# Attention, a dense layer and an expert layer in one planned kernel: V read in place, masks by sequence rows, early loads on two queues, and a searched table of due dates

## The chip, the cores and the metric

The kernel runs on one core of one Trainium2 chip. The metric is the device time of one launch in microseconds; the kernel before was run three times, and the median counts. Beside these runs stands one profiled execution, whose trace is read below. TensorE is called PE here, VectorE DVE, ScalarE ACT, GpSimd POOL and SyncE SP, as the profile calls them.

## The reference

Three layers follow each other. `_attn_ref` is a linear attention with a decaying state: batch 4, 8 heads, 768 positions, head size 48.

```python
for t in range(S):
    cur = einsum(u * k[t], v[t]);  y[t] = r[t] @ (state + cur)
    state = w[..., None] * state + outer(k[t], v[t])
```

`_moe_ref` is a dense layer on the 3072 tokens of 384 features: `softplus(x @ w_in) @ w_out` with 2048 hidden features. `_moe2_ref` gives every token to one of 8 experts: the scores `x @ w_gate` are taken in falling order and each expert holds 384 tokens; each expert computes `relu(x @ w1) @ w2` with 1024 hidden features.

## The kernel before

**The tiling.** Attention goes in 24 steps, each of 64 positions of two batches at once (128 partitions, 8 heads). A step loads K, R and V (`load_step`, L366, six DMAs into `KN`, `RN`, `VN`, each with two buffers), multiplies K and R by tables of the decay's powers (`PWN`), transposes both on PE (`tk` L497, `tq` L501), forms the 64x64 products of queries and keys (`prods`, L524), masks them (`masked`, L532 and L537), adds to the state (`fresh`, L558), and multiplies by V and by the state (`outs`, L607). For `outs` the masked products and the queries lie one above the other in a buffer `AR`, and V and the state lie one above the other in a buffer `X`, so that one matmul of 128 rows does both. V comes into `X` by copies from `VN` in the first six steps (`COPIED`), and by two more DMAs from memory later. The term with u is made by `sums` on PE (L591, with `rkT` from DVE, L586) in the first six steps (`TURNED`), and by four DVE operations (`bonus`) later. The result of the step (`xf`, L612) is transposed on PE (`tx`, L620) in the first six steps, and by a DMA transpose (`turn`, L623) later.

Three steps make a block of 384 tokens; there are eight. `ffn1` (L730) multiplies a block by w_in in 16 pieces (block 0 in float32, L743; the others in three float16 products, L748), and softplus runs on ACT and DVE. `ffn2` (L855 in float32 for block 0, L858 to L860 later) multiplies by w_out, which carries the gate's columns too. `late_logits` (L785, L786) makes the scores of the last tokens by small matmuls. Then the selection of the experts' tokens runs on DVE with small matmuls, and for each expert POOL gathers its rows, DMA transposes turn them (L1334), SP loads its weights in pieces (`mraw`, L1294), ACT and DVE split them, PE multiplies (L1346, then L1364 to L1366), and POOL scatters the result (L1374).

**The planner.** Nothing runs in the order in which it is written. Each piece of work is an `Item` with an engine (or a choice between ACT and DVE), an expected duration, its dependences and a due date. `lay_out` (L148) plays the program through with these durations before it is built: on each engine it takes, among the items that could start within `SLACK` of the earliest, the one that is due first, and the engines' instruction lists come out in that order. A transfer is an item of SP with a size in ns: its data are taken to land 1000 ns after a single serial DMA resource has worked off that size. Where the plan leaves PE idle, `keep_warm` (L135) writes matmuls on a tile of zeros, `still`, into PE's list (L143). They are instructions like all others: their number is fixed when the kernel is built.

```python
k = int((it.start - last - 100.0) / step)   # step: 107 ns before the first piece of work, 56 ns after
```

## Time and profile before

| what | value |
|---|---|
| three runs | 746.02, 747.25, 748.87 us; median 747.25 us |
| the profiled execution | 747.23 us, span of the trace 745.5 us |
| PE, DVE, ACT, POOL busy | 730.9, 610.0, 399.1, 61.2 us |
| granted TensorE clock, mean | 0.995 of 2.4 GHz |
| DMA | 79.06 MB, mean 106 GB/s |

The span runs from the first instruction's start to the last one's end; the profiled execution's own time is 1.7 us longer. A busy PE is one with a matmul in it; the matmuls on `still` count as busy, and overlap of neighbouring matmuls makes the busy time of one line longer than the time by which it moves the next one. That second time is read from the starts of two rows of a timeline.

### The profile page before, as it was taken

What the parts mean: (1) busy time and instruction counts of PE and PEld (TensorE: products, weight loads), DVE (VectorE), ACT (ScalarE), POOL (GpSimd) and SP (SyncE); (2) the same over time, 40 slices, a digit from 0 to 9 for tenths busy, and PEclk for the clock granted to TensorE, in tenths of its full rate; (3) what the DMA queues carried; (4) which work ended last, traced back from release to release, by engine and by line L of the source; (5) the groups of instructions that cost most, each with busy time, mean ns of one, the idle gap of its engine ahead of it and who ended that gap; (6) DMA issues with size and microseconds to landing.
All of it is one profiled execution on the core that took longest, in us unless ns stands there. A gap on an engine that the chain in (4) does not pass through costs nothing.

```text
span 745.5 us, 18249 instructions
## 1 busy us (share of the span) xinstructions
PE 730.9 (98%) x7196; PEld 475.0 (64%) x7196; DVE 610.0 (82%) x1663; ACT 399.1 (54%) x803; POOL 61.2 (8%) x100
## 2 busy tenths in 40 slices
PE   8899999999999999999999999999999999999996
PEld 7766666666666666667766665655655565656663
DVE  6899999999888788789998967887799799987530
ACT  4586776776565565667989901211235435433531
POOL 2000000000000000000001000000213312323211
PEclk9999999999999999999999999999999999999998
DMA  5796776135333233233110003342347647766910
GB/s 106 182 205 170 172 178 149 24 65 111 73 67 71 53 67 66 54 66 64 34 23 11 2 12 107 107 121 61 96 117 223 175 129 213 209 159 189 220 56 32
DMA packets 165013, 79.06 MB, mean 106 GB/s; under 512 B 130496, under 2 KB 160576, under 8 KB 164928
## 3 DMA queue, kind: packets, MB, share of 16 engines
q1 hardware_dynamic: 161856, 68.46, 39.6%
q0 software_dynamic: 3072, 9.44, 3.8%
q8 instruction: 56, 0.92, 0.5%
q14 instruction: 29, 0.24, 0.1%
HBM read 60.37 MB, written 9.83 MB: 94 GB/s over the span
## 4 chain that ended last, share of the span: by engine, by line
PE 68%; DVE 13%; issue 9%; ACT 3%; DMA 3%; POOL 2%; SPq 1%; POOLq 0%; DVEq 0%
PE bank L748 18%; PE bank L1346 8%; PE bank L858 7%; PE bank L860 7%; PE bank L859 7%; PE bank L855 3%; PE bank L607 2%; PE bank L1364 2%; PE bank L1365 2%; PE bank L1366 2%; PE bank L743 1%; DMA mraw<-moe_w 1%; DVE gf L761 1%; PE bank L524 1%; PE bank L558 1%
## 5 line engine op out<-in xcount | busy, mean ns | idle before, releaser
L748 PEld LDWEIGHTS <-wi 128*128 128x128 f16 x1008 | 97.8, 98 | 65.4 <-issue 2.0
L748 PE MATMUL bank<-xt,wi 128*128 128x384 f16 x672 | 127.6, 326 | 0.0
L754 ACT ACTIVATE ta<-bank 128x384 f32<-128x384 f32 x128 | 62.0, 484 | 65.4 <-PE bank L748 52.9
L858 PE MATMUL bank<-wo,g 128*128 128x384 f16 (+1 forms) x240 | 79.2, 330 | 0.0
L761 DVE SCALAR_TENSOR_TENSOR gf<-bank,ta 128x384 f32<-128x384 f32 x112 | 61.5, 550 | 21.6 <-ACT ta L756 20.8
L860 PE MATMUL bank<-wo,g 128*128 128x384 f16 (+1 forms) x240 | 79.1, 330 | 0.0
L859 PE MATMUL bank<-wo,g 128*128 128x384 f16 (+1 forms) x240 | 79.1, 329 | 0.0
L748 PE MATMUL bank<-xs,wi 128*128 128x384 f16 x336 | 72.9, 326 | 0.0
L1346 PE MATMUL bank<-g,w1h 128*128 128x384 f16 x384 | 72.9, 326 | 0.0
L755 ACT ACTIVATE ta<-ta 128x384 f32<-128x384 f32 x128 | 66.7, 521 | 2.8
L756 ACT ACTIVATE ta<-ta 128x384 f32<-128x384 f32 x128 | 66.7, 521 | 2.6
L1366 PE MATMUL bank<-w2h,g 128*128 128x384 f16 x192 | 62.6, 326 | 0.0
L1364 PE MATMUL bank<-w2h,g 128*128 128x384 f16 x192 | 62.6, 326 | 0.0
L1365 PE MATMUL bank<-w2l,g 128*128 128x384 f16 x192 | 62.6, 326 | 0.0
L1350 ACT ACTIVATE g<-bank 128x384 f16<-128x384 f32 x64 | 31.3, 489 | 44.9 <-PE bank L1346 30.9
L351 ACT ACTIVATE x2o<-bank 128x384 f16<-128x384 f32 x24 | 11.7, 488 | 78.7 <-PE bank L860 62.4
L1346 PEld LDWEIGHTS <-w1h 128*128 128x128 f16 x384 | 35.4, 97 | 23.1 <-issue 1.0
L1353 DVE SCALAR_TENSOR_TENSOR g<-bank,g 128x384 f16<-128x384 f32 x64 | 34.3, 547 | 15.0 <-ACT g L1350 14.9
L768 DVE SCALAR_TENSOR_TENSOR g<-gf,g 128x384 f16<-128x384 f32 x80 | 43.7, 551 | 1.9 <-ACT g L351 1.1
L1346 PE MATMUL bank<-g,w1l 128*128 128x384 f16 x192 | 41.7, 326 | 0.0
L537 DVE TENSOR_TENSOR ar<-bank,mask 64x256 f32<-64x256 f32 x84 | 35.4, 422 | 4.1 <-PE bank L524 2.4
L1269 POOL DMA_INDIRECT third<-x2d,idx x24 | 26.1, 1086 | 146.5 <-DVE si L1186 120.4
(232 smaller groups left out, 1448.8 us busy)
## 6 DMA issues: line engine op xcount, KB each, us to landing
mraw<-moe_w SPq DMA_DIRECT2D x64, 384.0 KB, 4.2
third<-moe_w_in SPq DMA_DIRECT2D x16, 384.0 KB, 4.3
third<-moe_w_out SPq DMA_DIRECT2D x8, 768.0 KB, 4.8
kn<-k SPq DMA_DIRECT2D x48, 96.0 KB, 3.0
rn<-r SPq DMA_DIRECT2D x48, 96.0 KB, 3.4
vn<-v SPq DMA_DIRECT2D x48, 96.0 KB, 3.0
x2d<-x2o SPq DMA_DIRECT2D x48, 96.0 KB, 2.2
X<-v SPq DMA_DIRECT2D x36, 96.0 KB, 3.1
```

Source lines behind the costliest of these rows:

```text
L748: PE.matmul(ph, WF[:, f, a, kk, :], x[:, kk, :], start=(i == 0), stop=(i == 3 * KC - 1))
L754: op("act", 371.0, lambda: ACT.activation(ta, bank.view(BT), AF.Abs), w=[("ta", c)], due=due, bank=bank)
L755: op("act", 413.0, lambda: ACT.activation(ta, ta, AF.Exp, scale=-1.0), w=[("ta", c)], due=due)
L756: op("act", 413.0, lambda: ACT.activation(ta, ta, AF.Ln, bias=1.0), w=[("ta", c)], due=due)
L761: op("dve", 470.0, lambda: DVE.scalar_tensor_tensor(gf, bank.view(BT), 0.0, ta, op0=OP.max, op1=OP.add), r=[("ta", c)], w=[("gf", c)], due ...
L858: PE.matmul(p, gh[:, f, ts], WU[:, f, 0, :no], start=(f == 0), stop=False)
L859: PE.matmul(p, gh[:, f, ts], WU[:, f, 1, :no], start=False, stop=False)
L860: PE.matmul(p, gl[:, f, ts], WU[:, f, 0, :no], start=False, stop=(f == FC - 1))
L1346: PE.matmul(ph, a[:, kk, fs], XH[p][:, x0 + kk, :], start=(i == 0), stop=(i == 3 * KC - 1))
L1364: PE.matmul(po, h1h[:, f, js], w2h[:, fz, :], start=(f == 0), stop=False)
L1365: PE.matmul(po, h1h[:, f, js], w2l[:, fz, :], start=False, stop=False)
L1366: PE.matmul(po, h1l[:, f, js], w2h[:, fz, :], start=False, stop=(f == FB - 1))
```

## The change

Six things are changed together.

1. **Steps 0 to 2** (`DIRECT`) no longer stack V and state. The products of both halves of the heads lie by sequence rows of all 128 partitions, so one mask multiplication of 128x256 per half of the heads takes the place of one of 64x512. `outs` multiplies the masked products by V where the load put it (16 matmuls of 64x48, `VN`), and in steps 1 and 2 adds 8 matmuls of the queries with the state (64x96, `X`, whose unused quarters are zeroed on POOL at the start). The copies of V into `X` fall away in these steps, the transposed queries are copied once instead of twice, and the sum with the u term is two DVE operations instead of one.
2. **Steps 3 to 5** (`TURNED` falls from 6 to 3) make the u term on DVE (`bonus`) and turn their result by a DMA transpose on SP, as the later steps did.
3. **Tables.** The power tables are made in fewer operations, the first products with K and R read them straight from PSUM, and `uw` is made on POOL.
4. **Loads.** Those of steps 0 to 2 (`QUEUES`) may be issued by ACT as well as by SP. R is loaded ahead of K.
5. **Block 0.** Its first eight pieces of `ffn1` (`PARTED`) are cut by step: three times three matmuls of 128 columns instead of three of 384.
6. **The planner.** A transfer now has two numbers by its kind (work of the serial resource, and time to landing after it), and two engines don't read one bank within `LAT` of each other. `SLACK`, `BIAS` and `YIELD0` are new values, and a table `NUDGE` moves the due dates of some 280 of the more than 3000 items of the plan.

The core of the diff (the same exchange of a size for a pair of numbers is left out where it repeats):

```diff
-    SLACK = 115.403
+    SLACK = 92.403
-    BIAS = 1.876
-    YIELD0 = 212.503
+    BIAS = 2.1139999999999994
+    YIELD0 = 118.0
+    ROWS = (610.0, 1850.0)
+    PIECE = (1520.0, 1420.0)
+    EXPERT = (1650.0, 1390.0)
+    GATHER = (620.0, 2400.0)
+    SCATTER = (640.0, 1000.0)
+    TURN = (1370.0, 700.0)
+    TURN2 = (1310.0, 1900.0)
+    NUDGE = {
+        2: 206418, 3: 1000001350, 55: -347751, 60: -114325, 69: 52946, 76: 72329, 90: -194834, 108: -43471, 109: -34113, 115: -1000280590,
...
+            for b in it.banks:
+                for e, t in b.last.items():
+                    if e != eng and eng != "pe":
+                        at = max(at, t + LAT)
...
-                dma = max(start + 1275.0, dma) + it.size
-                it.lat = dma + 1000.0 - it.done
+                dma = max(start + 1275.0, dma) + it.size[0]
+                it.lat = dma + it.size[1] - it.done
...
-    TURNED, TURN = 6, 1700.0
-    WHOLE = 3
+    TURNED = 3
+    DIRECT = 3
+    PARTED = 8
+    QUEUES = 3
...
-        for key, src, store in (("kn", k, KN), ("rn", r, RN), ("vn", v, VN)):
+        for key, src, store in (("rn", r, RN), ("kn", k, KN), ("vn", v, VN)):
             for b in range(2):
-                op("sp", 650.0, lambda b=b, src=src, store=store: SP.dma_start(
-                    store[i][b * 64:(b + 1) * 64], src[b0 + b, :, s0:s0 + C, :].rearrange("h s d -> s h d")),
-                    w=[(key, i, b)], due=due, size=640.0)
+                def load(eng=None, b=b, src=src, store=store):
+                    (ACT if eng == "act" else SP).dma_start(
+                        store[i][b * 64:(b + 1) * 64], src[b0 + b, :, s0:s0 + C, :].rearrange("h s d -> s h d"))
+
+                op({"sp": 650.0, "act": 650.0} if n < QUEUES else "sp", 650.0, load, w=[(key, i, b)], due=due, size=ROWS)
+        if n < DIRECT:
+            return
...
+        if direct:
+            op(FROM_BANK, 0.0, lambda eng: copied(eng, rT, b2.view(HP, 128)), w=[("ar", i, 0), ("ar", i, 1)], due=due + 2, bank=b2)
...
         def masked(q):
+            if direct:
+                DVE.tensor_mul(am[:, q], b3[q].view(HP, 64), mask[:, None, :].to_broadcast([128, HP, 64]))
+                return
...
         def outs():
+            if direct:
+                py = [b.view(H, D) for b in b55]
+                for h in range(H):
+                    for b in range(2):
+                        rows = slice(b * 64, (b + 1) * 64)
+                        PE.matmul(py[b][rows, h, :], am[rows, h % 2, h // 2, :], VN[i][rows, h, :], start=h == 0, stop=h == H - 1 and n % PC == 0)
+                for b in range(2 if n % PC else 0):
+                    for pr in range(HP):
+                        PE.matmul(py[b][b * 64:(b + 1) * 64, 2 * pr:2 * pr + 2, :], rT[:, pr, b * 64:(b + 1) * 64], X[x][:, :, b, pr, :],
+                                  start=False, stop=pr == HP - 1)
+                return
...
+        def part(t, m):
+            ts = slice(t * 128, (t + m) * 128)
+            for kk in range(KC):
+                PE.matmul(bank.view(BT)[:, ts], WF32[f][:, kk, :], X32[:, kk, ts], start=(kk == 0), stop=(kk == KC - 1))
...
-    total = lay_out(items, lambda it: (it.prio, it.n), {"sp": 1000.0, "dve": 900.0}, True)
+    total = lay_out(items, lambda it: (it.prio + NUDGE.get(it.n, 0), it.n), {"sp": 1000.0, "dve": 900.0}, True)
```

What the planner makes of it is seen in the engines' lists. Three places follow; a name's number is its buffer (`kn_93` and `kn_94` are the two buffers of K), and an "x" the count.

**ACT, from the program's start.** Before, its first work after the load of its function table is the copy of a power table out of PSUM:

```order
L241 ACT_TABLE_LOAD
L357 COPY pwn_147<-bank_80 128x512
L357 COPY X_97<-vn_95 64x192
L357 COPY pwn_146<-bank_81 128x512
L357 COPY kT_109<-bank_82 128x512
```

and now:

```order
L287 ACT_TABLE_LOAD
L426 DMA kn_94<-k 64x8x48
L426 DMA rn_91<-r 64x8x48 x2
L426 DMA kn_93<-k 64x8x48
L426 DMA vn_95<-v 64x8x48
L426 DMA rn_92<-r 64x8x48
L426 DMA kn_94<-k 64x8x48
L426 DMA vn_96<-v 64x8x48
L409 COPY kT_110<-ar_112 128x8x32
L409 COPY pwn_146<-bank_80 128x512
```

Eight issues of transfers now stand ahead of the copy of half of a power table, and that copy ahead of the first transposes on PE.

**PE, `outs` of the second step.** Before, in the first step (the later ones are the same), it is one row of 16 matmuls on `X` between `fresh` and the next step's `prods`:

```order
L558 MATMUL bank_84<-vn_96,ks_103 64x48
L558 MATMUL bank_85<-vn_96,ks_103 64x48
L607 MATMUL bank_86<-X_97,ar_111 64x48 x16
L524 MATMUL bank_80<-ar_112,kT_110 64x64
```

and now, in the second step:

```order
L842 MATMUL bank_86<-xt_117,wi 128x128 x3
L184 LDWEIGHTS still
L184 MATMUL bank_87<-still 128x128
L679 MATMUL bank_84<-vn_96,ar_112 64x48
L679 MATMUL bank_85<-vn_96,ar_112 64x48
L682 MATMUL bank_84<-X_98,ar_112 64x96 x4
L682 MATMUL bank_85<-X_98,ar_112 64x96 x4
L661 MATMUL bank_83<-uw,xhl 128x2 x4
```

The first row is a third of a piece of `ffn1` of block 0: it stands ahead of the second step's `outs`, where before no row of `ffn1` stood ahead of the third step's transposes. The matmuls of 64x48 read `vn_96` itself.

**PE, between the last two experts.** Before, the last matmul of one expert and the first of the next have 41 pairs on `still` between them (one is shown):

```order
L1366 LDWEIGHTS g_128
L1366 MATMUL bank_82<-w2h,g_128 128x384
L143 LDWEIGHTS still
L143 MATMUL bank_87<-still 128x128
L1346 LDWEIGHTS w1h
L1346 MATMUL bank_83<-g_129,w1h 128x384
```

and now none:

```order
L1473 LDWEIGHTS g_128
L1473 MATMUL bank_84<-w2l,g_128 128x384
L1474 LDWEIGHTS g_128
L1474 MATMUL bank_84<-w2h,g_128 128x384
L1454 LDWEIGHTS w1h
L1454 MATMUL bank_81<-g_129,w1h 128x384
```

In the whole list of PE, the matmuls on `still` fall from 270 to 183. Up to the first float16 matmul of `ffn1` they were 185 and are 149; from there to the end they were 85 and are 34. Of the other rows, those of `sums` fall from 24 to 12 and those of `tx` from 18 to 9, 24 matmuls of 384 columns become 72 of 128, and 48 of the 384 of `outs` become 48 of 64x48 and 16 of 64x96.

## Rows read from the trace of the kernel before

**Rows 1.** The page: PE's busy time, share and instructions.

```profile
PE 730.9 (98%) x7196; PEld 475.0 (64%) x7196; DVE 610.0 (82%) x1663; ACT 399.1 (54%) x803; POOL 61.2 (8%) x100
```

**Rows 2.** Busy time by stretches, all engines; then clock, DMA share, GB/s.

```profile
0.00:5.00 5.00, 4.00 (x45) 4.00 (x46) 1.53 (x13) 1.28 (x1) 4.16 (x17) 1.00 0.26 39
...
35.00:100.00 65.00, 63.41 (x683) 43.38 (x682) 62.39 (x122) 46.92 (x101) 0.00 (x0) 1.00 0.79 184
```

**Rows 3.** What PE waited for, whole span: us in total, times, longest.

```profile
PE bank L743 <- DVE wi L659: 1.4, 2, 1.0
PE bank L558 <- DVE ks L346: 1.4, 1, 1.4
```

**Rows 4.** Matmuls on `still` (L143) by stretches: length, PE busy (count), PEld busy.

```profile
0.00:6.50 6.50, 4.75 (x55) 4.57 (x55) 1.00 0.39 64
6.50:34.20 27.70, 6.43 (x81) 5.46 (x81) 1.00 0.74 165
34.20:100.00 65.80, 4.70 (x52) 3.43 (x51) 1.00 0.78 182
100.00:400.00 300.00, 4.82 (x22) 2.15 (x22) 1.00 0.34 69
400.00:700.00 300.00, 1.60 (x20) 1.17 (x20) 0.99 0.46 128
700.00:745.50 45.50, 2.45 (x41) 2.37 (x41) 0.96 0.30 72
```

**Rows 5.** Timeline of PE before the last expert: start, length, what.

```profile
712.97 2.45 PE L143 MATMUL bank<-still 128*128 128x128 bf16 x41
...
715.26 1.14 PE L1346 MATMUL bank<-g,w1h 128*128 128x384 f16 x6
```

**Rows 6.** Timeline of SP: the last expert's DMA transposes.

```profile
701.27 2.59 SPq L1334 DMA_TRANSPOSE g<-third  x2
```

**Rows 7.** PE's groups of 0 to 34.2 us, by shape: busy us, mean ns.

```profile
L524 PE MATMUL bank<-ar,kT 64*64 64x64 f32 x128 | 4.5, 223 | 0.0
L607 PE MATMUL bank<-X,ar 128*64 128x48 f32 x96 | 3.8, 225 | 0.5 <-DVE ar L532 0.4
...
L558 PE MATMUL bank<-vn,ks 64*64 64x48 f32 x128 | 2.7, 222 | 1.4 <-DVE ks L346 1.4
...
L620 PE MATMUL bank<-identf,xf 128*128 128x128 f32 x9 | 1.6, 285 | 0.4 <-DVE xf L612 0.3
```

**Rows 8.** Timeline of PE, first 45 us.

```profile
23.37 0.66 PE L497 MATMUL bank<-identf,ks 128*128 128x128 f32 x4
23.86 0.49 PE L620 MATMUL bank<-identf,xf 128*128 128x128 f32 x3
...
32.17 0.69 PE L524 MATMUL bank<-ar,kT 64*64 64x64 f32 x32
...
37.52 1.05 PE L591 MATMUL bank<-uw,xhl 128*128 128x2 f32 x8
38.44 4.12 PE L743 MATMUL bank<-xt,wi 128*128 128x384 f32 x12
42.39 0.49 PE L620 MATMUL bank<-identf,xf 128*128 128x128 f32 x3
```

**Rows 9.** Timeline of all engines, first 8 us.

```profile
0.74 1.28 ACT L241 ACT_TABLE_LOAD   x1 [0.74 <-PEq L1460]
...
1.93 1.42 SPq L373 DMA_DIRECT2D kn<-k  x2
...
5.80 0.43 DVE L359 COPY kT<-ar 128x512 f32<-128x512 f32 x1
...
7.04 0.59 ACT L357 COPY pwn<-bank 128x512 f32<-128x512 f32 x1 [5.02 <-PE bank L465]
```

**Rows 10.** PE alone by stretches: length, busy (count), granted clock.

```profile
431.00:434.00 3.00, 3.00 (x21) 0.50 0.00 0
```

**Rows 11.** DVE's groups, whole span: busy us, mean ns.

```profile
L346 DVE TENSOR_TENSOR rk<-rk,ut 128x384 f32<-128x384 f32 x18 | 9.9, 548 | 0.2
```

More of the change, by code (lines that the diff above doesn't have):

```diff
@@ L79, in tile_kernel, with __init__ @@
     class Item:
-        def __init__(self, eng, dur, fn, deps, prio, lat=LAT, take=None, bank=None, size=0.0):
+        def __init__(self, eng, dur, fn, deps, prio, lat=LAT, take=None, bank=None, size=None):
             self.eng, self.dur, self.fn, self.prio, self.lat = eng, dur, fn, prio, lat
@@ L95, in __init__ @@
             self.cls, self.slot, self.items, self.all = cls, None, [], []
+            self.last = {}
         def view(self, *dims, dtype=None):
@@ L107, in view, with op @@
             return t
-    def op(eng, dur, fn, r=(), w=(), due=0.0, lat=None, bank=None, size=0.0, small=False):
+    def op(eng, dur, fn, r=(), w=(), due=0.0, lat=None, bank=None, size=None, small=False):
         deps = []
@@ L440, in powers @@
         DVE.reciprocal(rec, sq[:, 5])
-        DVE.tensor_mul(pw[:, :, :C // 2], t, rec[:, :, None].to_broadcast([128, HP, C // 2]))
         DVE.tensor_mul(sq[:, 6], sq[:, 5], sq[:, 5])
@@ L483, in attention @@
         rnk, knk, vnk = [[(a, i, b) for b in range(2)] for a in ("rn", "kn", "vn")]
-        product(ks[:, :, :D], KN[i], PWN[1][:, :, :D], knk + [("pwn", 1), "pads"], [("ks", i)], due)
-        product(rs[:, :, :D], RN[i], PWN[0][:, :, :D], rnk + [("pwn", 0), "pads"], [("rs", i)], due + 1)
-        if n % PC == 0:
+        if n:
+            product(ks[:, :, :D], KN[i], PWN[1][:, :, :D], knk + [("pwn", 1), "pads"], [("ks", i)], due)
+            product(rs[:, :, :D], RN[i], PWN[0][:, :, :D], rnk + [("pwn", 0), "pads"], [("rs", i)], due + 1)
+        direct = n < DIRECT
+        if n % PC == 0 and not direct:
             def zero():
@@ L517, in prods @@
         def prods():
-            pa = None if n < WHOLE else [b.view(HP, 64) for b in b3]
             for pr in range(HP):
@@ L585, in attention @@
         if n < TURNED:
-            op("dve", 602.0, lambda: DVE.tensor_tensor(rkT, b2.view(HP, 128), kT, op=OP.mult), r=[("kT", i)], w=["rkT"],
-               due=due + 3, bank=b2)
+            op("dve", 602.0, lambda: DVE.tensor_tensor(rkT, rT if direct else b2.view(HP, 128), kT, op=OP.mult),
+               r=[("kT", i)] + ([("ar", i, 0)] if direct else []), w=["rkT"], due=due + 3, bank=None if direct else b2)
             def sums():
@@ L640, in attention @@
             op("sp", 700.0, turn, r=[("xhl", i, 0), ("xhl", i, 1)], w=[("xh", g, t), ("xl", g, t), ("x2", g, t)], due=due + 5, size=TURN)
[L641 removed]
+        op({"act": 413.0, "dve": 200.0}, 0.0, lambda eng: scaled(eng, h2, hi, 2.0 ** -11),
            r=[("xh", g, t)], w=[("x2", g, t)], due=due + 5)
@@ L737, in ffn1 @@
         ta, gf = TA[c], GF[c]
+        def part(t, m):
+            ts = slice(t * 128, (t + m) * 128)
+            for kk in range(KC):
+                PE.matmul(bank.view(BT)[:, ts], WF32[f][:, kk, :], X32[:, kk, ts], start=(kk == 0), stop=(kk == KC - 1))
         def mm():
             ph = bank.view(BT)
-            if blk == 0:
-                for kk in range(KC):
-                    PE.matmul(ph, WF32[f][:, kk, :], X32[:, kk, :], start=(kk == 0), stop=(kk == KC - 1))
-                return
             i = 0
@@ L838, in tile_kernel @@
         X2S.append(op("sp", 650.0, lambda row=(b0 + i % 2) * S + s0: SP.dma_start(x2d[row:row + 64, :], none),
-                      r=["none"], due=begins(0) + 5000.0, size=273.0))
+                      r=["none"], due=begins(0) + ZERODUE, size=STORE))
     def ffn2(blk, t, late=False):
@@ L888, in tile_kernel @@
         load_step(n)
+        if n == 0:
+            for i in range(2):
+                power_table(i)
         attention(n)
```

140 lines of the change are left out of this document (90 added, 50 removed), and 27 rows, old and new, of the table NUDGE.

## The prediction

> **What bounds the kernel now.** I read the page first: PE is busy 98% of the span [rows 1]. Then I asked what PE waits for, because a PE that waits much would make the other engines the subject; but its two longest sums are 1.4 us each [rows 3]. So PE's own instruction list sets the time, and a change is worth what it takes out of that list plus what it does to the waits. The list is not all work: 270 matmuls on `still` stand in it, 24.8 us busy in all, as the six stretches of [rows 4] add up. What one of them costs is read where 41 stand in a row: from their first start to the next row's is 715.26 - 712.97 = 2.29 us, 56 ns each [rows 5]. They are instructions, so PE runs them whether it would have had to wait or not. Before the last expert it would not: the transposes that bring this expert's input are issued by 701.27 + 2.59 = 703.9 us [rows 6], nine microseconds ahead of those fillers. That is the reader's key to this change: a planned wait is paid for in full, even where the real one never comes.
>
> By stretches DVE is the second engine to watch: from 35 to 100 us it is busy 62.39 of 65 us [rows 2]. In the first 5 us the DMA engines carry 39 GB/s against 184 GB/s from 35 to 100 us [rows 2].
>
> **The change, part by part.** A float32 matmul counts as two in the trace.
>
> *Products* (steps 0 to 2). Four steps' products stand ahead of 34.2 us, 4.5 us busy [rows 7]; the fourth is already of the form that all have now and takes 0.69 us [rows 8]. The three others take (4.5 - 0.69) / 3 = 1.27 us each, so 3 x (1.27 - 0.69) = 1.7 us go.
>
> *`outs`* (steps 0 to 2) is 3.8 us now [rows 7]. Afterwards each has the number and shape of matmuls that `fresh` has, 2.7 / 4 = 0.68 us [rows 7], and two of them 8 more of 64x96, 16 in the trace. No row shows that shape. A float32 matmul of 384 columns takes (42.39 - 38.44) / 12 = 0.33 us [rows 8], so 96 columns are 0.08 us; if two halves of the array work side by side, as the 0.68 / 32 = 21 ns of a matmul in `fresh` suggests, 16 take 0.66 us, if not 1.3 us. I take the first: 3 x 0.68 + 2 x 0.66 = 3.4, a gain of 0.4 us; the other end is a loss of 0.9 us.
>
> *`sums`* of steps 3 to 5 goes: 38.44 - 37.52 = 0.92 us each [rows 8], 2.8 us. *`tx`* of these steps goes: 1.6 / 3 = 0.53 us busy [rows 7]; less the 0.13 us by which a row overlaps the next, as 1.05 against 0.92 us in `sums`, that is 0.40 us, 1.2 us for three.
>
> *Block 0 in parts.* 24 matmuls of 384 columns are 48 in the trace and 48 x 0.33 = 15.8 us. Cut, they are 144 of 128 columns. The nearest row of float32 matmuls of 128 columns with new weights for each is the transposes: (23.86 - 23.37) / 4 = 0.12 us [rows 8], 17.6 us; by columns alone it would be 15.8 us. A loss between 0 and 1.8 us; I take 0.6.
>
> These five make 1.7 + 0.4 + 2.8 + 1.2 - 0.6 = **5.5 us** less work on PE. None of it needs cover: it leaves the list of the engine that is the bound.
>
> *Fillers.* 270 - 183 = 87 go, 87 x 0.056 = **4.9 us**. 36 of them stood ahead of the first float16 matmul of `ffn1`, 51 later. For this to be a gain, the work that follows must be ready without them. At the experts it was, as shown above; in the head the plan expects it to be ready because the first thirds of `ffn1` fill the place.
>
> *What moves to DVE, ACT and SP.* `bonus` adds four operations of 0.548 us [rows 11] to each of steps 3 to 5, 6.6 us on DVE in the stretch where it has 2.6 us free [rows 2]. Against that DVE loses the product `rkT` and the sum from PSUM in these steps, the wider masks and most of the V copies. I cost the balance at nothing; if DVE falls behind there, PE is late by that much, for no filler is left to hide it. The DMA transposes of steps 3 to 5 wait on SP for DVE, and the loads of w_out and of the next steps are queued behind them.
>
> *ACT's issues.* An issue costs SP 1.42 / 2 = 0.71 us [rows 9]. If it costs ACT the same and begins after the function table (0.74 + 1.28 = 2.0 us [rows 9]), the eight end at 7.7 us. ACT had nothing to do until 7.04 us [rows 9], which hides most of it; but the copy behind them is needed by the first transposes, whose power table DVE had finished by 5.80 + 0.43 = 6.2 us [rows 9]. So the first real work of PE starts between 0 and 1.6 us later, and 0.3 us more for ACT's own copy if all goes badly. I take a loss of **1.0 us**: the issues are certain, and a queue that the trace shows issuing back to back on SP has no reason to be quicker on ACT.
> The Trainium skill (DMA: Bandwidth & Descriptors, section Issuing engines are not separate DMA queues) says that transfers from several engines share the same 16 DMA engines and that issuing on several saves only the issuing time. The trace agrees that there is issuing time to save: the DMA engines are 0.26 busy in the first 5 us [rows 2]. By the rule the term would be a gain, not a loss, as the first rival works out from rows.
>
> **The sum.** 5.5 + 4.9 - 1.0 = 9.4 us less. Against the profiled execution's 747.23 us that is 737.8, and I write **738.0 us**; the median of the runs, 747.25 us, is the same number for this purpose. A measurement of this kernel can tell about 0.5%, that is 3.7 us, from no change.
>
> One cost may vanish or stay by chance: after the small matmuls of `late_logits`, which come as one run of 136 and another of 56 before, PE's granted clock is at 0.50, the lower level of 1.2 GHz, for 3 us [rows 10], which costs about half of that, 1.5 us. They now come as 24 earlier and then 112, 32 and 24. I leave the cost in the sum and its loss in the range.
> The Trainium skill (TensorE: Matmul & The Clock Gate, section HAM oscillation — how this bites in real kernels) says that a matmul engine which is left idle falls to the lower clock and must be kept busy to stay at the higher. By that rule taking out fillers risks more than the waits themselves. The rule is weighed in the last rival.
>
> **The rivals.**
>
> *The plan holds and real waits shrink too* (0.25). The transfers are now planned with numbers nearer to the landings, so loads come when they are wanted; the 1.4 us that `fresh` waited for K's product [rows 3] and the clock's 1.5 us go as well, and ACT's issues cost nothing: 738.0 - 1.4 - 1.5 - 1.0 = 734 us. If SP's back-to-back issues are what holds the head, the eight that ACT takes over are even worth up to 8 x 0.71 = 5.7 us: 747.23 - 5.5 - 4.9 - 5.7 = 731 us, 0.03 of the 0.25; the first transposes wait for a power table and not for a load, so I give it no more. For the case speaks that the last expert's fillers were a pure planning loss. Against it: a wait that is taken away at one place uncovers the next.
>
> *Half comes back as new waits* (0.14). Due dates searched against a table of durations leave no slack; where an operation is late, PE now idles. V read in place is one such place: `VN` is not free for the load of step 2 until the `outs` of step 0, which reads it, so that load's issue, on ACT, holds the copies behind it. A wait of some 1.5 us at each of three or four places gives 743 to 745 us. For it speaks DVE's 62.39 of 65 us; against it, that the old order ran in the same full stretch with PE waiting under 3 us [rows 3].
>
> *DVE falls behind in the full stretch* (0.04), the one that ends slower. If the 6.6 us of `bonus` were not paid for by what DVE loses, and the transposes of steps 3 to 5 held SP's queue for as long again, block 1 of `ffn1` would start late and w_out with it. It decides when these waits come to more than 9.4 us plus the 3.7 us that can be told: 13 us. With 6.6 us of DVE, 6.6 us of queue by that assumption, and a clock at 0.50 behind each wait for as long as in [rows 10] (three times 1.5 us), it is 17.7 us: 747.2 - 9.4 + 17.7 = 755.5 us. Against it: the removed work of DVE is about as large, and loads run ahead by two buffers.
> The rule on the idle engine stands behind the clock's part of it; without it the case gives 751 us, just past the point.
>
> *The change does not do what it says* would mean the same order with other constants. The lists exclude that: 87 fillers and three forms of work are gone. Its rest of chance (0.02) is with no change.
>
> **How the numbers follow.** The forecast has 0.55: 735.5 to 741 us by the bounds of its terms (`outs` 1.3 up, parts 1.2 up and 0.6 down, ACT 0.9 up and 1.0 down, clock 1.5 down). The two neighbours reach 733 and 745. A range of **732.5 to 744 us** leaves out some 0.15: the upper end of the third case, the slower one, and a little below. Faster by over 0.5% is under 743.5 us: 0.55 + 0.25 and half of 0.14, **0.87**. Within 0.5%: the rest of the third case and the last, **0.09**; slower **0.04**.
>
> **What would show it.** Right: 183 matmuls on `still`, none between the last two experts, and `outs`, products and `sums` together some 5 us below; PE's waits still under 10 us in all; ACT's first copy near 7.7 us. Wrong: waits of PE on DVE or a DMA between 35 and 110 us that sum to several microseconds, a low clock outside the run of small matmuls, or a first matmul of `ffn1` block 0 that starts no earlier than before.

## The result and the profile after

The changed kernel takes 737.35 us, the median of four runs (737.19 to 737.50); the kernel before beside it 747.20 us (746.02 to 748.87). The ratio is 0.9867, 95% interval 0.9847 to 0.9886. The prediction was 738.0 us. The profiled execution took 737.29 us, its span is 735.5 us.

The page's first part, as [rows 1]:

```profile
PE 721.0 (98%) x7204; PEld 473.8 (64%) x7204; DVE 608.3 (83%) x1658; ACT 392.2 (53%) x799; POOL 64.1 (9%) x107
```

PE still stands at 98%. Where the time went is seen if the span is cut at the same places of the program: half a microsecond ahead of the last float16 matmul of `ffn1`, at the first small matmul of the selection, at the first matmul of the first expert and at that of the last. The columns are those of [rows 2]; the first two of the five stretches are shown, the lengths of all stand in the table below. Before:

```profile
0.00:425.20 425.20, 418.39 (x4684) 282.86 (x4685) 373.14 (x882) 295.47 (x627) 7.15 (x28) 1.00 0.42 88
425.20:443.60 18.40, 18.40 (x290) 12.83 (x289) 13.20 (x46) 3.43 (x8) 0.00 (x0) 0.91 0.04 9
...
```

And after:

```profile
0.00:419.80 419.80, 412.58 (x4765) 285.05 (x4766) 371.03 (x875) 288.57 (x625) 9.25 (x35) 1.00 0.44 91
419.80:437.90 18.10, 18.10 (x270) 12.48 (x269) 13.32 (x47) 3.08 (x7) 0.00 (x0) 0.91 0.05 13
...
```

5.4 us went from attention and dense layer, 0.3 from the stretch with the low clock, 1.8 from the selection, 2.5 from the experts up to the last, and nothing behind it. This cut is used for every run below, and the four moving stretches are called dense, clock, selection and experts. The gain of the dense stretch is made early. To the end of block 0 in `ffn1` it is 84.3 us before and 78.6 us after, and both PE and DVE are busy some 6 us less in that time:

```profile
0.00:84.30 84.30, 78.52 (x1051) 59.93 (x1051) 73.15 (x165) 53.20 (x111) 4.23 (x17) 1.00 0.75 170
```

```profile
0.00:78.60 78.60, 72.08 (x1051) 61.26 (x1052) 67.23 (x145) 46.91 (x101) 6.33 (x24) 1.00 0.91 194
```

The experts' 2.5 us are almost one place. Timeline of PE after, as [rows 5]: the last expert follows the one before without a row between.

```profile
705.14 0.33 PE L1474 MATMUL bank<-w2h,g 128*128 128x384 f16 x1
705.30 0.98 PE L1454 MATMUL bank<-g,w1h 128*128 128x384 f16 x5
```

The matmuls on `still` by stretches, as [rows 4], one of the six (behind 700 us there is none):

```profile
6.50:34.20 27.70, 5.36 (x58) 4.17 (x58) 1.00 0.99 204
```

What PE waited for, as [rows 3]: 7.2 us in five rows, and the first two are new and not small.

```profile
PE bank L527 <- ACT kT L409: 3.3, 1, 3.3
PE bank L597 <- ACT kT L409: 2.0, 1, 2.0
PE bank L184 <- DVE ar L489: 1.0, 1, 1.0
```

By stretches, as [rows 2]: the transfers now fill twice as much of the first 5 us, and from 35 to 100 us PE never idles, with DVE at 98%.

```profile
0.00:5.00 5.00, 3.99 (x41) 4.00 (x42) 1.07 (x9) 1.28 (x1) 3.94 (x17) 1.00 0.52 87
...
35.00:100.00 65.00, 64.99 (x758) 49.28 (x757) 63.95 (x122) 48.47 (x111) 0.00 (x0) 1.00 0.88 205
```

The changed forms on PE, as [rows 7, 8]. Timeline of the third step: `fresh`, and then the two halves of the new `outs`:

```profile
30.66 0.68 PE L628 MATMUL bank<-vn,ks 64*64 64x48 f32 x32
31.16 1.11 PE L679 MATMUL bank<-vn,ar 64*64 64x48 f32 x32
32.20 1.26 PE L682 MATMUL bank<-X,ar 128*64 128x96 f32 x16
```

`outs` with the shape and the count of `fresh` takes 1.1 us, not 0.68.

The head's new wait, as [rows 9]. Timeline of ACT, first 10 us:

```profile
0.75 1.28 ACT L287 ACT_TABLE_LOAD   x1 [0.75 <-PEq L1568]
0.78 0.71 ACTq L426 DMA_DIRECT2D kn<-k  x1
1.52 1.33 ACTq L426 DMA_DIRECT2D rn<-r  x2
2.90 0.76 ACTq L426 DMA_DIRECT2D kn<-k  x1
3.71 0.63 ACTq L426 DMA_DIRECT2D vn<-v  x1
6.07 0.60 ACTq L426 DMA_DIRECT2D rn<-r  x1
7.28 0.60 ACTq L426 DMA_DIRECT2D kn<-k  x1
8.32 0.60 ACTq L426 DMA_DIRECT2D vn<-v  x1
8.96 0.40 ACT L409 COPY kT<-ar 128x256 f32<-128x256 f32 x1 [6.93 <-DMA vn<-v]
```

The issues begin beside the table load, five go back to back, and then ACT stands. The chain of waits of this stretch says on what (start, length):

```profile
2.90 4.36 DMA kn<-k
7.26 0.02 issue
7.28 5.47 DMA kn<-k
...
12.77 0.57 DVE ks L398
...
13.37 0.60 ACTq L426
```

The second buffer's K is issued 0.02 us after the first one's has landed, though the two have nothing to do with each other. The compiled list of ACT has the reason (its rows 4 to 9 follow, a row's number ahead): every transfer reports to one of eight completion semaphores, handed out in turn over both queues, and its issue waits until the transfer that had that semaphore before has landed.

```
4 L426 DMA kn_93<-k 64x8x48 [waits DMAHW0_49]
5 L426 DMA vn_95<-v 64x8x48 [waits DMAHW2_49]
6 L426 DMA rn_92<-r 64x8x48 [waits DMAHW6_49]
7 L426 DMA kn_94<-k 64x8x48 [waits DMAHW0_49]
8 L426 DMA vn_96<-v 64x8x48 [waits DMAHW2_49]
9 L409 COPY kT_110<-ar_112 128x8x32 [waits DVE_49]
```

By 3.40 us the two queues have handed out all eight, and a load of K, R or V landed some 4 to 5 us after its issue. So ACT's copy starts at 8.96 us and PE's first transposes at 9.46. The chain's last row is a later issue on ACT, which waits for DVE to be done with the buffer, and behind it stands the copy for which PE waits 2.0 us: the place that the second rival named, with R's buffer instead of V's.

### The profile page after: what moved, and what is told of

It reads as the page before. It is cut to its first block, busy times and chain, and to the rows that moved or that the text cites. A ratio compares the mean times of both kernels' runs of the same rounds, so it can differ in the third digit from the quotient of the medians.

```text
span 735.5 us, 18327 instructions
## 1 busy us (share of the span) xinstructions
PE 721.0 (98%) x7204; PEld 473.8 (64%) x7204; DVE 608.3 (83%) x1658; ACT 392.2 (53%) x799; POOL 64.1 (9%) x107
## 4 chain that ended last, share of the span: by engine, by line
PE 75%; issue 10%; DVE 6%; POOL 3%; DMA 3%; ACT 3%; ACTq 0%; POOLq 0%; DVEq 0%
PE bank L849 21%; PE bank L963 8%; PE bank L964 7%; PE bank L965 7%; PE bank L842 4%; PE bank L1454 4%; PE bank L960 3%; PE bank L689 3%; PE bank L597 2%; PE bank L1472 2%; PE bank L570 2%; PE bank L1474 2%; PE bank L1473 2%; POOL out L1482 1%; DMA mraw<-moe_w 1%
## 5 line engine op out<-in xcount | busy, mean ns | idle before, releaser
L859 ACT ACTIVATE ta<-bank 128x384 f32<-128x384 f32 x128 | 61.1, 479 | 19.4 <-PE bank L849 13.0
L1411 DVE SCALAR_TENSOR_TENSOR w2l<-mraw,w2h 128x768 f16<-128x768 f32 x32 | 30.4, 954 | 12.5 <-ACT w2h L1407 12.4
```

Source lines behind the costliest of these rows:

```text
L859: op("act", 371.0, lambda: ACT.activation(ta, bank.view(BT), AF.Abs), w=[("ta", c)], due=due, bank=bank)
```

## The experiments

The stretches of all profiled runs, in us (edges as above); in the last column the median of the runs without a profile and with it.

| run | dense | clock | selection | experts | rest | median (range) |
|---|---|---|---|---|---|---|
| before | 425.2 | 18.4 | 95.5 | 176.2 | 30.2 | 747.20 (746.02 to 748.87) |
| after | 419.8 | 18.1 | 93.7 | 173.7 | 30.2 | 737.35 (737.19 to 737.50) |
| after, again (e5) | 420.2 | 19.4 | 93.8 | 173.3 | 30.2 | 736.39 (735.48 to 738.63) |
| five loads on ACT (e1) | 419.3 | 16.8 | 94.6 | 173.3 | 30.2 | 737.97 (736.00 to 739.37) |
| after, 49 matmuls on still out (e2) | 421.9 | 16.8 | 94.5 | 174.0 | 30.2 | 738.54 (736.59 to 739.19) |
| before, 133 out (e3) | 424.9 | 18.0 | 95.6 | 174.5 | 30.2 | 744.96 (743.10 to 747.36) |
| after without the table (e4) | 424.0 | 18.0 | 95.8 | 176.3 | 30.2 | 746.89 (744.25 to 748.63) |
| 6.5 us more on DVE (e6) | 428.2 | 17.9 | 93.7 | 173.2 | 30.2 | 746.78 (744.64 to 749.09) |
| 6.6 us more on PE (e7) | 427.8 | 16.8 | 93.7 | 172.9 | 30.2 | 744.29 (742.98 to 746.33) |
| three loads behind ACT's copy (e9) | 419.6 | 19.4 | 94.6 | 173.4 | 30.2 | 738.81 (737.74 to 739.82) |
| six loads on POOL (e10) | 420.4 | 19.4 | 94.7 | 173.4 | 30.7 | 740.30 (738.40 to 742.11) |
| stores on ACT (e11) | 417.7 | 16.8 | 94.5 | 174.3 | 30.2 | 735.35 (734.33 to 739.19) |
| stores later (e12) | 417.4 | 16.7 | 93.8 | 173.8 | 30.2 | 736.47 (733.71 to 739.11) |

### What is a matmul on `still` worth? (e2, e3)

Both runs have one edit, which stops the writing of these matmuls at a planned time:

```diff
-    WARM = 1e9
+    WARM = 34000.0
```

In the changed kernel it takes out 37 of the dense stretch and 12 of the selection:

> The changed kernel without the matmuls on the zero tile behind the plan's 34th microsecond: 49 of 183 go, nothing else moves. Theory A (they are paid for in full, since PE would not have to wait there): 49 x 0.056 = 2.7 us less, 734.6 us, up to 736.3 - 3.6 = 732.7 if the change of shape around the single ones goes too. Theory B (they only fill waits that are there anyhow): 737.4 us and 2.7 us more in PE's waits. Theory C (without them PE's clock falls): slower than 737.4, with stretches at a granted clock of 0.50 that the changed kernel does not have.

Not faster: 738.54 us, ratio to before 0.9863 (0.984 to 0.9886), and the dense stretch of the profiled run is 2.1 us longer. But the edit didn't cost this time. Up to 42 us the run has the same matmuls on `still` as the changed kernel; the first one that it lacks stood at 48.23 us there. Matmuls on `still` by stretches of this run (the changed kernel has the same 58 in the first stretch, see above), and behind them the changed kernel's second one:

```profile
6.50:34.20 27.70, 6.62 (x58) 5.17 (x58) 0.82 0.98 203
...
42.00:100.00 58.00, 0.00 (x0) 0.00 (x0) 1.00 0.87 206
```

```profile
42.00:100.00 58.00, 2.21 (x16) 1.23 (x16) 1.00 0.91 215
```

All that the run loses it loses ahead of that point, in two stretches at the lower level of the clock:

```profile
10.60:14.00 3.40, 3.40 (x31) 3.03 (x32) 1.80 (x4) 0.79 (x2) 0.00 (x0) 0.50 1.15 237
...
17.40:24.30 6.90, 6.90 (x115) 6.00 (x115) 4.85 (x12) 2.53 (x6) 0.00 (x0) 0.51 0.82 140
```

The changed kernel itself has such a stretch in its second profiled run (e5, 0.50 from 10.7 to 14.1 us). What the 37 matmuls were worth is read behind 42 us, from two rows that the changed kernel (first) and this run both have:

```profile
48.38 0.68 PE L628 MATMUL bank<-vn,ks 64*64 64x48 f32 x32
...
418.95 0.65 PE L849 MATMUL bank<-xt,wi 128*128 128x384 f16 x3
```

```profile
51.21 0.68 PE L628 MATMUL bank<-vn,ks 64*64 64x48 f32 x32
...
421.11 0.65 PE L849 MATMUL bank<-xt,wi 128*128 128x384 f16 x3
```

The run is 2.83 us late at the first and 2.16 at the second: 37 matmuls, 2.1 us by 0.056 each, gave 0.7 us. It is one profiled run beside one other, and the two of the changed kernel differ by 0.3 us over the same stretch.

In the kernel before the same edit takes out 72 in the dense stretch, 17 in the selection, and 44 among the experts, 41 of them ahead of the last:

> The kernel before without the matmuls on the zero tile behind the plan's 34th microsecond: 133 of 270 go, nothing else moves. Theory A (paid in full): 133 x 0.056 = 7.4 us less, 739.8 us (738 to 741), the 41 ahead of the last expert alone 2.3 us. Theory B (they fill real waits): 747 us. Theory C (the clock falls without them): slower than 747, with new stretches at 0.50.

744.96 us, ratio 0.9958 (0.9944 to 0.9972), some 3 us for 133 matmuls. By stretches: the dense one, without 72 matmuls, 4.0 us of PE, is 0.3 us shorter; 17 gave nothing in the selection. The last expert begins 23.4 us behind the one before it (689.6 to 713.0) instead of 25.7 (689.6 to 715.3): 41 matmuls gave 2.3 us, just 41 x 0.056. The 0.3 us isn't theirs: at block 0's first matmul of `ffn1`, where none is missing yet, the run is already 0.7 us early (33.54 us; 34.27 before). From there on it loses and gains. Timeline of PE before, and of this run with its clock:

```profile
52.86 1.11 PE L143 MATMUL bank<-still 128*128 128x128 bf16 x17
54.95 2.20 PE L743 MATMUL bank<-xt,wi 128*128 128x384 f32 x6 [0.98 <-DVE wi L659]
```

```profile
54.21 3.90 PE L743 MATMUL bank<-xt,wi 128*128 128x384 f32 x6 [2.03 <-DVE wi L659]
...
54.40:57.80 3.40, 3.40 (x6) 1.51 (x5) 3.28 (x8) 2.01 (x5) 0.00 (x0) 0.50 0.72 223
```

Seventeen matmuls stood in a wait for a piece of w_in. Without them PE idles there for 2.0 us, and the next six matmuls run at a clock of 0.50 and take 3.9 us instead of 2.2. Behind it the run gains: 0.8 us late against the kernel before at 60 us, 0.3 us early at the last float16 matmuls, 1.2 us for the 52 matmuls (2.9 us) taken out there. So both readings hold, each at its place: at the last expert the planned wait never came and the matmuls were paid for in full; in the dense stretch a third to two fifths of their length came back, and in this run a fall of the clock took more than that.

### What is the searched table worth? (e4)

```diff
-    total = lay_out(items, lambda it: (it.prio + NUDGE.get(it.n, 0), it.n), {"sp": 1000.0, "dve": 900.0}, True)
+    total = lay_out(items, lambda it: (it.prio, it.n), {"sp": 1000.0, "dve": 900.0}, True)
```

The plan then writes 284 matmuls on `still`, 24 of them ahead of the last expert but one.

> The changed kernel without the table that moves single due dates; all else as in the changed kernel, so the planner makes another order, with 284 matmuls on the zero tile instead of 183. Theory A (the length of PE's list sets the time, and the search is worth what it takes out of it): 101 x 0.056 = 5.7 us more, 743 us (741.5 to 746). Theory B (a searched order has no slack and gives its gain back in waits, the unsearched one has fewer): 737 to 740 us, with PE's own waits several microseconds below those of the changed kernel, 8.2 us.

746.89 us, ratio 0.999 (0.9974 to 1.0005): without the table the change is worth nothing that can be told. It is 4.2 us slower in the dense stretch than the changed kernel, 2.1 in the selection and 2.6 among the experts. That is more than its 101 matmuls (5.7 us; 69 of them, 3.9 us, stand in the dense stretch). PE's waits in sight don't make the difference, they are 6.3 us against 7.2. A part may be the clock, at 0.50 from 8.5 to 15.3 us in this profiled run; the rest is open. With the same forms on PE, the dense stretch is only 1.2 us shorter than before, but it has 240 matmuls on `still` where the kernel before had 209. The new values of `SLACK`, `BIAS` and `YIELD0` stayed in; whether others would serve better without the table was not tried. What the table would do for the kernel before was not tried, since its numbers count other items.

### Which engine holds the head? (e5, e6, e7)

The changed kernel once more, and two kernels with more work in steps 3 to 5 that the planner doesn't know of: on DVE,

```diff
-lambda: DVE.tensor_reduce(sd, rk, axis=AX.X, op=OP.add)
+lambda: [DVE.tensor_reduce(sd, rk, axis=AX.X, op=OP.add) for _ in range(5 if n < 6 else 1)]
```

and on PE, behind the products:

```diff
+            for _ in range(39 if 3 <= n < 6 else 0):
+                PE.matmul(banks[7][:, :128], still, still, start=True, stop=True)
```

> The changed kernel itself, unaltered, beside the next runs on one chip: 737.4 us by every theory. It gives the time from which the two extra loads of work are counted.

> In steps 3 to 5 the reduction of the u term is done five times instead of once (same result, same order of everything else; the plan does not know of it): 12 more operations of 0.54 us on DVE (the row of that line after the change), 6.5 us, between about 33 and 70 us. Theory A (PE's list sets the time and DVE's work beside it is covered, as the prediction had it): 737.4 to 738.5 us. Theory B (from 20 to 140 us DVE, busy 9.8 of every 10 us, holds the head as much as PE): 743 to 744 us.

> The same weight on the other side: 39 more matmuls on still behind the products of each of steps 3 to 5, 117 x 0.056 = 6.6 us of PE in the same stretch. Theory A (PE's list sets the time): 744 us. Theory B (DVE holds the head and PE has cover behind it): 737.4 to 738.5 us. If both engines are full, this and the run with more work on DVE both cost several microseconds.

736.39, 746.78 and 744.29 us (ratios 0.9853, 0.999 and 0.9964; intervals 0.9831 to 0.9875, 0.9975 to 1.0006, 0.995 to 0.9977). Neither theory alone: 6.5 us on DVE lengthen the dense stretch by 8.0 us, 6.6 us on PE by 7.6, and the medians are 10.4 and 7.9 us above e5. Both engines hold it. Windows of 20 to 140 us, of the changed kernel, then with more on DVE, then with more on PE:

```profile
20.00:140.00 120.00, 119.63 (x1506) 89.78 (x1500) 117.15 (x238) 86.48 (x195) 0.00 (x0) 1.00 0.71 161
```

```profile
20.00:140.00 120.00, 114.07 (x1421) 85.13 (x1412) 115.61 (x231) 80.21 (x183) 0.00 (x0) 0.99 0.68 155
```

```profile
20.00:140.00 120.00, 119.63 (x1562) 92.17 (x1558) 111.09 (x222) 81.66 (x185) 0.00 (x0) 1.00 0.73 156
```

PE is busy 119.6 of 120 us and DVE 117.2; what is added to one turns up as idle time of the other, 5.6 us of PE in the second row, 6.1 us of DVE in the third. What each stretch costs beyond that has another source in its run. With more on DVE, the last of the three additions ends in waits of PE of 1.5 and 0.5 us at 85 to 87 us, and behind them the clock is at 0.50, which loses another 1.6 us (first two rows; why the median lies higher still is open). With more on PE, the run is 6.5 us behind the changed kernel's first profile from 73 us on, just what was added; another 1.4 us comes at 271 us, where a load of R is late for DVE (last row; the run with loads on POOL, e10, loses as much at the same place):

```profile
86.20 0.33 PE L810 MATMUL bank<-identf,third 128*128 128x128 f32 x1 [1.49 <-ACT third L409]
...
87.70:91.10 3.40, 3.40 (x6) 1.69 (x5) 3.40 (x6) 2.08 (x4) 0.00 (x0) 0.50 0.71 134
```

```profile
269.13 0.56 DVE L398 TENSOR_TENSOR rk<-rn,kn 128x384 f32<-128x384 f32 x1 [1.65 <-DMA rn<-r]
```

### Why is `outs` no cheaper? (e8)

Ahead of the first transposes stand four groups of 32 float32 matmuls of 64x48 (each 64 in the trace), results unused, on one, two and four positions of the array, and 128 rows deep on its two column halves:

```diff
+                for j in range(32):
+                    PE.matmul(two[0][0:64, :48], identf[0:64, 0:64], identf[0:64, 0:48], start=True, stop=True)
+                for j in range(32):
+                    a = slice(j % 2 * 64, j % 2 * 64 + 64)
+                    PE.matmul(two[j % 2][a, :48], identf[a, 0:64], identf[a, 0:48], start=True, stop=True)
+                for j in range(32):
+                    a, c = [slice(z * 64, z * 64 + 64) for z in (j % 2, j // 2 % 2)]
+                    PE.matmul(two[j % 2][c, :48], identf[a, 0:64], identf[a, 0:48], start=True, stop=True)
+                for j in range(32):
+                    c = slice(j % 2 * 64, j % 2 * 64 + 64)
+                    PE.matmul(two[0][c, :48], identf[:, 0:64], identf[:, 0:48], start=True, stop=True)
```

> 128 extra float32 matmuls of 64x48 ahead of the first transposes, in four groups of 32 (64 records each), their results unused: all on one position of the array; alternating between two that share neither rows nor columns (as outs of the first steps now); going round four (as fresh); and 128 rows deep on two column halves (as outs of the later steps). Theory P (positions work side by side, so outs lost its gain by using two): per 32 matmuls four positions 1.37 us (twice the 0.68 of fresh), two about 2.1 to 2.2, one 4 or more. Theory Q (outs is slow for another reason, its operands or its banks): two positions as fast as four, 1.4 us. The time itself is 4 to 9 us longer and tells nothing.

Timeline of PE in this run (start, length), the four groups in this order and what follows:

```profile
5.81 3.72 PE L528 MATMUL bank<-identf 64*64 64x48 f32 x61
...
9.41 1.99 PE L531 MATMUL bank<-identf 64*64 64x48 f32 x62
...
11.27 1.11 PE L534 MATMUL bank<-identf 64*64 64x48 f32 x61
12.31 2.07 PE L537 MATMUL bank<-identf 128*64 128x48 f32 x64
14.32 0.66 PE L540 MATMUL bank<-identf,kT 128*128 128x128 f32 x4
```

From start to start: 3.60, 1.86, 1.04 and 2.01 us for the 61, 62, 61 and 64 matmuls of a row (the few others of a group stand between the rows). Theory P, each size a little under what it gave. Half as many positions cost nearly twice the time: 59, 30 and 17 ns a matmul. `outs` before used two positions 128 rows deep (31 ns); now it has a diagonal pair of four (30 ns); `fresh` goes round all four. There was no time to be gained.

### What is ACT's hold at the start worth? (e1, e9, e10, e11, e12)

First five of the eleven loads stay on ACT, the other six go back to SP (e10 to e12 build on this count; a list tells each load its queue when it is written out, and the plan stays as it was):

```diff
-                    (ACT if eng == "act" else SP).dma_start(
+                    (ACT if eng == "act" and EARLY_ACT.pop() else SP).dma_start(
```

> The changed kernel, in which ACT issues its first five loads only; the six later ones stand at the same place of the order but are issued by SP. Theory A (the loads of both queues take turns on eight completion semaphores, so from the ninth load on each issue waits for a landing, and ACT's copies stand behind these waits): ACT's copy of the half power table starts near 6.5 us instead of 8.96, the first transposes on PE near 7.0 us instead of 9.46, and the wait of 2.0 us that PE has for ACT's copy of kT before the first products goes: 2.5 + 2.0 = 4.5 us less, 733 us (731.5 to 734.5). Theory B (an issue costs ACT its 0.65 us and nothing more; the head's waits are of the data): the copy moves by less than 0.5 us and the time stays at 737. Theory C (the head is not on the path, later waits take it back): the first transposes move to 7 us, and the time stays at 736 to 737.5.

ACT's copy starts at 5.78 us, the first transposes at 6.63 instead of 9.46, 2.8 us earlier, and the first part of `ffn1` at 17.1 instead of 21.5. Yet the dense stretch ends only 0.5 us earlier, and the time is 737.97 us, ratio 0.987 (0.9847 to 0.9893). Timeline of this run, rows of SP and DVE:

```profile
24.55 0.58 SPq L467 DMA_DIRECT2D ut<-u  x1
...
29.57 0.56 DVE L399 TENSOR_TENSOR rk<-rk,ut 128x384 f32<-128x384 f32 x1 [1.63 <-DMA ut<-u]
```

SP, with six issues more, is late with u (24.55 us; 23.01 in the changed kernel) and with w_in, and DVE waits 1.63 us for the one and at 32.41 us 1.35 for the other. The next run leaves SP's list alone and puts only three issues behind ACT's copy:

```diff
+                        if 6 <= ISSUED[0] <= 8:
+                            LATER.append(go)
+                            return
...
             ACT.copy(o, a)
+            while LATER:
+                LATER.pop(0)()
```

> The changed kernel with one edit to ACT's list: the sixth to eighth load are issued behind ACT's first copy instead of ahead of it. SP's list is untouched. First transposes on PE at 6.6 us (9.5 to 9.7 before the edit) by every theory; ACT's next copies still stand behind the three issues. Theory S (in the run with five loads on ACT the early start was eaten by SP's queue, which issued the six moved loads ahead of the load of u and the pieces of w_in): with SP's list as it was, the last float16 matmul of ffn1 comes 1 to 2 us earlier than in the unaltered kernel (420 us), time 735 to 736 us. Theory F (what ACT holds up at the start is caught up later in any case, because the stretch behind it is filled by PE and DVE together with other loads as the limit): within 0.5 us of it, 736.4 to 737.4 us.

Theory F by the dense stretch, which is 0.2 us shorter; the time, 738.81 us, ratio 0.9865 (0.9839 to 0.9892), is above what either theory gave. First transposes at 6.64 us, but the second step's K is still issued late, and DVE stands in front of it until 13.25 us (12.77 in the changed kernel):

```profile
13.25 0.56 DVE L399 TENSOR_TENSOR ks<-kn,pwn 128x384 f32<-128x384 f32 x1 [2.21 <-DMA kn<-k]
```

So the hold costs through the loads behind it, not through the copy. With the six on POOL:

```diff
-                    (ACT if eng == "act" else SP).dma_start(
+                    (SP if eng != "act" else [SP, ACT, POOL][EARLY_ACT.pop()]).dma_start(
```

> The changed kernel with ACT's first five loads left on ACT and its six later ones issued by POOL. SP's list is untouched, ACT has no issue behind its first copy. First transposes at 6.6 us. If an issue on POOL waits for the landing eight issues earlier too, POOL stands still, which has nothing else to do then but the clearing of X and uw. Theory S: the whole early start is kept as far as DVE's 98% allows, last float16 matmul of ffn1 2 to 3 us earlier than 420 us, time 733.5 to 735 us. Theory F: 736.4 to 737.4 us. A third case: loads that POOL issues land later than SP's, and DVE waits for them: 738 us or more.

740.30 us, ratio 0.9885 (0.9856 to 0.9913): the third case's size by another way. POOL issued the first three without a hold (4.36, 6.17, 6.86 us), but the granted clock was 0.72 from 10 to 20 us, and why it fell there is open. Even so the run is 0.8 us ahead of the changed kernel from 34 to 260 us. The dense stretch comes out 0.6 us longer because 1.4 us are lost near 264 us, behind a wait of DVE of 1.58 us ahead of the operation that waits for R in e7; the loads on POOL were long over there. Last, the four stores of zeros to the experts' output leave SP, first to ACT where they stood (the edit shown), then to ACT from 30 us on:

```diff
-        X2S.append(op("sp", 650.0, lambda row=(b0 + i % 2) * S + s0: SP.dma_start(x2d[row:row + 64, :], none),
+        X2S.append(op("sp", 650.0, lambda row=(b0 + i % 2) * S + s0: ACT.dma_start(x2d[row:row + 64, :], none),
```

> As the run with five loads on ACT and six on SP, but the four stores of zeros to the experts' output go from SP to ACT, so that SP has two issues more than in the changed kernel instead of six. Theory S: between the two, the load of u is issued near 23.5 us instead of 24.6, time 735.5 to 737 us. Theory F: 736.4 to 738 us as with five on ACT.

> As the run with five loads on ACT and the four stores of zeros on ACT, but the stores come one by one behind ACT's copies from about 28 us on, outside the stretch in which the second and third step's loads are under way. Theory S (the stretch of 10 to 40 us is held by the loads that SP issues, and each transfer less there lets the next one go sooner): last float16 matmul of ffn1 at 417 us or before (417.7 with the stores early on ACT, 420 in the changed kernel), time 734 to 735.5 us. Theory F (what is gained in the head is caught up by DVE and PE, both at 98% from 20 us): 735.4 to 737.4 us. If the stores hold up ACT's copies and softplus there, 738 us.

735.35 and 736.47 us (ratios 0.9837, 0.9805 to 0.987, and 0.9848, 0.982 to 0.9876). In the profiled runs the dense stretch ends at 417.7 and 417.4 us, 2.1 and 2.4 earlier than in the changed kernel, which fits theory S (417 us, though not its time of 734 to 735.5): what holds the head's first 40 us are the loads, those of the second step and SP's behind them, more than ACT's copy. In the whole time it is not to be told from the changed kernel, whose runs spread from 735.48 to 738.63 in one set alone. No run shows a version that surely beats it.

## Why the prediction was right

The time was 0.65 us off, and faster came as said. The steps behind it did not all hold.

*PE's list sets the time.* Half of it. What is added to PE costs its full length (e7), but what is added to DVE does too (e6); from 20 to 140 us there are two lists that both run at 98% or more. DVE was costed at nothing, and that came out well because DVE's work fell too: to the end of block 0 it is busy 67.2 us instead of 73.2, as much less as the stretch is shorter. A part of that work only moved behind this point: over the dense stretch it is 371.0 us instead of 373.1. No run takes the one gain without the other, so how much of the head's gain is owed to each list isn't shown.

*The five terms.* From each row's start to the next one's, summed over a form, PE spent on the products 17.37 us before and 15.63 after, on `sums` 5.28 and 2.56, on `tx` 2.13 and 1.15, on block 0 31.83 and 32.20, on `outs` 27.99 and 27.73. That looks like 5.3 us where 5.5 were forecast. But this measure gives a wait to the row ahead of it: `outs` before holds 1.9 us of waits, the 1.4 us of [rows 3] among them, and `fresh`, whose matmuls have not changed, holds 2.0 us of them after (13.69 us before, 15.17 after). Without the waits the products lose 1.7 us (predicted 1.7), `sums` 2.7 (2.8), `tx` 1.0 (1.2), block 0 gains 0.4 (0.6), and `outs` gains 1.6 where it was to lose 0.4: 3.4 us in all, 2.1 short of the forecast.

*`outs` is the term whose working failed.* "Each has the number and shape of matmuls that `fresh` has" took the price from the wrong row. The new work is 3 x 1.11 + 2 x 1.26 = 5.9 us against 3.8 before [rows 7], past the far end of the bounds. `fresh` goes round four positions of the array and the new `outs` round two, and e8 shows what that costs.

*The matmuls on `still`.* "A planned wait is paid for in full, even where the real one never comes" holds at the last expert, 2.3 of the 4.9 us. Elsewhere, taken out by themselves, they gave a third to two fifths of their length (e2, e3), and in the old head nothing in the end, since behind a wait that they had filled the clock fell (e3). "None of it needs cover" for the five terms isn't shown either way: without the table the dense stretch is 1.2 us shorter than before (e4), with 31 more of these matmuls in it and a low clock in the head.

Counted like the terms, from start to start without the waits, the dense stretch closes: 3.4 us of the terms and 2.0 us of 38 matmuls on `still` make its 5.4; the waits are 0.4 us longer, and the other rows 0.4 us shorter.

*ACT's issues.* An issue took 0.6 to 0.76 us, as sized (0.71). The step that failed is "the eight end at 7.7 us": they end at 8.92, since three of them wait for earlier landings. PE's first wait grew from 0.6 to 3.3 us and one of 2.0 us came with it, against a term of 1.0 (the prediction's rows give 1.5 us, not 1.6, for the far end of it, and its bounds add up to 734.9 to 741.4 us, not 735.5 to 741; neither decides anything). Over the whole span PE's pauses did not grow for all that: the span less PE's busy time is 14.6 us before and 14.5 after [rows 1]. In the end the copy's delay was worth half a microsecond at most (e1, e9), since the loads behind it held the head anyway; with those freed as well it was 2.4 us of the dense stretch (e12).

The Trainium skill (DMA: Bandwidth & Descriptors, section Issuing engines are not separate DMA queues) let this term come out as a gain, the time of issuing saved. The trace speaks against that here: the second queue saved issuing time and brought PE waits of 3.3 and 2.0 us.

*What was not in the sum.* The selection became 1.8 us shorter, and without the table it did not (e4: 95.8 us); with the same table it lay between 93.7 and 94.7. This was not predicted. Of it 0.5 us is no gain but a shift: three matmuls of `ffn2` now run ahead of the cut, in the stretch with the low clock (363 of 128x384 stand behind it instead of 366; 366 again in e4), and 0.3 us is five matmuls on `still`; the cause of the rest was not looked for. The clock's dip stayed, as written down: 0.91 over its stretch before and after.

The last rival's clock appeared behind PE's waits, though not in the changed kernel's first profiled run: 0.50 from 54.4 us behind a wait of 2.0 us (e3), and from 87.7 us behind waits of 1.5 and 0.5 (e6). The Trainium skill (TensorE: Matmul & The Clock Gate, section HAM oscillation — how this bites in real kernels) says that a wait of the matmul engine can bring its clock down, so that the work behind it starts slow. These two runs agree. The first run of the changed kernel shows that it need not come: PE waited 3.3 us in the head, and the clock stayed at 1.00 until 424 us.

So the sum of 9.4 us for 9.9 is partly luck. The five terms were 2.1 us short, and ACT's 1.0 us isn't seen in the sum of PE's pauses, which stayed as it was; the selection's 1.8 us make up for the rest. What the prediction said one would see if it were right was there in most points: 183 matmuls on `still` and none ahead of the last expert, PE's waits under 10 us, and a first matmul of block 0's `ffn1` that starts earlier (21.54 us, 34.27 before). Two points were not: ACT's first copy came at 8.96 us instead of near 7.7, and `outs`, products and `sums` together are 4.7 us below with the waits counted, but 2.8 without.

## What to carry to other kernels

Before an engine is called the bound, look at how full the second is in the same stretch, and add a few microseconds to each: where both cost their length, dummy work taken off PE alone gave back a third to two fifths here. A dummy matmul is worth its full length only where the trace shows the work behind it ready; elsewhere it may fill a wait behind which the clock falls. Before a loss in one profiled run is put down to an edit, look whether it stands behind the first instruction that the edit changed. Take the price of a small matmul from a row that uses the same positions of the array, not only the same shape.

## What the runs showed of the hardware

- Small float32 matmuls of 64x48 took 59, 30 and 17 ns on one, two and four positions of the array, and 31 ns on two positions 128 rows deep (e8).
- Transfers of two queues share eight completion semaphores in turn, so an issue on one queue waited for a landing of the other: 6.07, 7.28 and 8.32 us on ACT, the second of them 0.02 us behind the landing at 7.26.
- PE's clock fell to 0.50 behind waits of 2.0 us (e3, at 54.4 us) and of 1.5 and 0.5 us (e6, at 87.7 us), and took 1.6 to 1.7 us each time. With 17 matmuls on `still` and 0.98 us of waiting in the first of these places it stayed at 1.00 (the kernel before).
- One program, twice: behind PE's wait for ACT's first copy the granted clock from 10 to 20 us was 1.00 in one profiled run (wait 3.3 us) and 0.83 in the other (3.9 us). The stretch with the small matmuls took 16.7 to 19.4 us over the runs of the changed kernel's order, with the work in it unchanged. Much of the scatter of this kernel may lie in these two places; that was not tried.
